# Column products over one pre-added tile in place of four, in a spectral MLP layer on one core: POOL adds the squares, ACT and POOL build two modulation rows

## The chip, the cores and the metric

The kernel runs on one core of a Trainium2 chip. The metric is the time of one execution on the device, in microseconds (us). Engines are named as in the profile: PE (matrix products; PEld is its weight load), DVE (vector), ACT (scalar and activation functions), POOL (the general-purpose SIMD engine), SP (it issues the DMAs). Each engine works through its own instructions in the order in which the program holds them; between engines, semaphores make one wait for another.

## The reference

One layer with adaptive normalisation, a spectral block and a gated MLP, over 8192 positions of 448 channels. Cut to what matters:

```python
mod = (silu(c) @ w_mod).reshape(1, 6, 1, -1)
sa, ca, ga, sb, cb, gb = (mod[:, q] for q in range(6))     # six rows of 448
h = layernorm(x) * (1 + ca) + sa
x = x + ga * A(h, w1, b1, w2, b2)     # rfft over positions, a complex two-layer block MLP, irfft
h = layernorm(x) * (1 + cb) + sb
x = x + gb * ((gelu(h @ w_gate) * (h @ w_up)) @ w_down)    # w_gate, w_up: 448 x 1792
```

The kernel computes `w_gate` and `w_up` products in 16-bit halves, for which it scales the weights by powers of two. To choose these it wants an upper bound on the norm of every column of `w_gate` and `w_up` (`nrm`: sums of squares down the 448 rows).

## The kernel before, in words

There are three stages, one after the other. The first (to about 95 us in the trace) reads `x`, normalises it and does the first part of the transform; its result goes to DRAM (`td`). The second (about 95 to 407 us) is the spectral block. The third is the gated MLP, in which PE is busy nearly all the time.

The change lies in the second stage. It treats 32 units (a half `h` of the channels and one of 16 groups `bt` of frequencies) in a software pipeline. `step(i)` works on several units at once, and the order of its calls is the order of the instructions on every engine (the scheduler is switched off here):

- `fetch_t(i+2)`: SP issues the loads of a unit (`tr`), then the hook "load"
- the hook "pe", which stands ahead of all other PE work of the step
- `stage_s2(i)`: PE makes the second transform (`ps`, L344 to L346, 24 products); ACT (`zh`, L352) and DVE (`zl`, L353) write it as two halves
- `split_t(i+1)`: ACT writes `th` and POOL writes `tl` for the next unit
- the hook "act"
- `stage_m2(i-2)`, twice: PE makes the second MLP layer (`pm`, L417 to L422, 12 products each time); DVE clips it (`t`, L430) and writes `y` (L438); `split_y` lets ACT write `yh` (L99) and POOL write `yl` (L101)
- `stage_i1(i-3)`: PE makes the inverse transform (`pi`, L467 to L469); ACT copies it (`us`, L470), and SP stores it (`vd`)
- the hook "dve"
- `stage_m1(i-1)`: PE makes the first MLP layer (`pm`, L390 to L395, 24 products); ACT (`hh`, L407) and DVE (`hl`, L408) write it as two halves
- the hook "pool", which stands behind all other POOL work of the step

The function `at(i, hook, fn, ...)` hangs side work into these hooks. In steps 1 to 16 this is the work on the weights' norms. `load_w` brings 256 columns of `w_gate` or `w_up` (`raw`: 448 rows as three tiles of 128 rows and one of 64, that one twice). One step later `squares` (ACT, L633) writes the squares in bf16 (`sq`, four tiles of 256 columns). Another step later `norms` multiplies each tile's columns with a column of ones on PE (L642, 4 tiles by 2 halves of 128 columns are 8 products) and adds them up in PSUM (`pw`); `norms_out` (DVE, L649) scales the sum by a bound's margin. There are 14 such pieces, in steps 3 to 16.

`mod_row` makes a modulation row, the same on all 128 partitions: for each half of 224 columns, four f32 products of silu(c) (`cs`), spread over 128 columns, with the four tiles of 112 rows of `w_mod` (L606, 8 products; the trace shows an f32 product as two, so 16). It stands in the hook "pe" of step 6 for the row `cb` and of step 8 for `sb`; ACT copies the result (L609). The rows `ga` and `gb` are made after the loop in the same way.

The tiles `raw` come from a pool of eight buffers and `sq` from four.

Of the kernel before, what the change touches and what calls it, by code (L numbers as in the profile page):

```python
# [10 lines left out]
F32 = mybir.dt.float32  # L11
# [4 lines left out]
AF = mybir.ActivationFunctionType  # L16
ALU = mybir.AluOpType
# [6 lines left out]
HC = 224  # L24
# [17 lines left out]
def spectral_geglu(ctx, tc, x, w1, b1, w2, b2, wg, wu, wd, cvec, wmod, cf1, cs2, cmi, cgm, out):  # L42
    nc = tc.nc
    V, S, G, T = nc.vector, nc.scalar, nc.gpsimd, nc.tensor
# [9 lines left out]
    cpool = ctx.enter_context(tc.tile_pool(name="cpool", bufs=1))  # L54
    psum = ctx.enter_context(tc.tile_pool(name="psum", bufs=2, space=bass.MemoryType.PSUM))

    def bank(tag, name):
        return psum.tile([128, 512], F32, tag=tag, name=name)
# [4 lines left out]
    make_identity(nc, ident)  # L63
    onesb = cpool.tile([128, 2], BF16, name="onesb")
    V.memset(onesb, 1.0)
    ga_r = cpool.tile([128, D], F32, name="ga_r")
    gb_r = cpool.tile([128, D], F32, name="gb_r")
    cb_r = cpool.tile([128, D], F32, name="cb_r")
    sb_r = cpool.tile([128, D], F32, name="sb_r")
    cs = cpool.tile([112, 4], F32, name="cs")  # L70
    nrm = cpool.tile([128, 2, NFT], F32, name="nrm")
# [56 lines left out]
    with ExitStack() as actx:  # L128
# [18 lines left out]
        q, y, t, nm, mu = (ap.tile([128, NB], F32, name=nm) for nm in ("q", "y", "t", "nm", "mu"))  # L147
# [117 lines left out]
        pe, start = 0.0, {}  # L265
        for g, bs in enumerate(groups):
# [5 lines left out]
            at = [pos[0] + 0.06] + [pos[i] + d for i in (1, 2, 3) for d in (0.03, 0.06)] + [pos[3] + 0.1]  # L272
            if g == 0:
                at = [t_stats[e] + 0.2] + [pos[0] + 0.03] * 7
            for t_, f in zip(at, scale_steps(bs)):
                ex(t_, f)
            for bb in bs:
                pe = start[bb] = max(pe + 0.75, at[-1] + 0.3)
# [20 lines left out]
    with ExitStack() as bctx:  # L299
# [200 lines left out]
        def at(i, hook, fn, *args):  # L500
            side.setdefault((i, hook), []).append((fn, args))
# [80 lines left out]
        raws = {}  # L582
# [16 lines left out]
                out.append(wm)  # L599
            return out  # L600

        def mod_row(key, dst=None):
            ps = bank("pd", "psm")
            for hh, wm in enumerate(raws.pop(key)):
                for k in range(4):
                    T.matmul(ps[:, hh * HC : (hh + 1) * HC], cs[:, k : k + 1].to_broadcast([112, 128]), wm[:, k, :], start=k == 0, stop=k == 3)  # L606
            if dst is None:
                return ps[:, :D]
            S.copy(dst, ps[:, :D])  # L609
# [21 lines left out]
        def squares(pr, j):  # L631
            sq = npool.tile([128, 4, 256], BF16, tag="sq", name="sq", bufs=4)
            S.activation(sq, raws.pop(("n", pr, j)), AF.Square)  # L633
            raws[("q", pr, j)] = sq

        def norms(pr, j):
            sq = raws.pop(("q", pr, j))
            ps = bank("pd", "pw")
            for f in range(2):
                for t in range(4):  # L640
                    kr = 128 if t < 3 else 64
                    T.matmul(  # L642
                        ps[:, f : f + 1], sq[:kr, t, f * 128 : (f + 1) * 128], onesb[:kr, 0:1], start=t == 0, stop=t == 3
                    )
            raws[("s", pr, j)] = ps

        def norms_out(pr, j):
            ps = raws.pop(("s", pr, j))
            V.tensor_scalar(nrm[:, pr, 2 * j : 2 * j + 2], ps[:, 0:2], 1.02, 1e-30, op0=ALU.mult, op1=ALU.add)  # L649

        def all_max(dst, src, n, first=(), then=()):

# [100 lines left out]

        nctx = ExitStack()
        npool = nctx.enter_context(tc.tile_pool(name="npool", bufs=1))
        at(3, "load", pre, npool, "cb", load_mod_row, 4)
        at(5, "load", pre, npool, "sb", load_mod_row, 3)
        at(6, "pe", mod_row, "cb", cb_r)
        at(8, "pe", mod_row, "sb", sb_r)
        for n in range(14):  # L760
            j, pr = divmod(n, 2)
            at(1 + n, "load", pre, npool, ("n", pr, j), load_w, pr, j)
            at(2 + n, "act", squares, pr, j)
            at(3 + n, "pe", norms, pr, j)
            at(3 + n, "pe", norms_out, pr, j)
        for j in range(7):
# [106 lines left out]
        drain()  # L873
        down_weights(0, G)
        mod_row("ga", ga_r)
        assert not tiny
    mctx.close()
# [406 lines left out]
```

## Time and profile before

| | |
|---|---|
| median of 3 runs | 2001.53 us (2000.57 to 2001.66) |
| the profiled execution | 2000.8 us |
| its span in the trace | 1999.0 us |
| PE busy | 1928.4 us, 96% of the span |
| DVE, ACT, POOL busy | 1155.3, 769.1 and 1198.8 us |
| mean granted clock of PE | 0.985 of full speed |

The span is what the trace covers; the execution's own time lies 1.8 us above it, and 0.7 us under the median. The busy shares are means over three stages that have different limits, so the table alone does not say what a change in the second stage is worth.

### The profile page before, as it was taken

To read this page: it belongs to the slowest core of one execution; us is meant where nothing else is said; L and a number is where in the kernel's file an instruction comes from. 1 tells how busy PE (TensorE), PEld (TensorE's weight loads), DVE (VectorE), ACT (ScalarE), POOL (GpSimd) and SP (SyncE) were. 2 spreads that over 40 slices of the span, in tenths; PEclk is the share of its full clock that TensorE was granted. 3 is DMA by queue.
4 is the path that set the end of the run, shared out by engine and by line. 5 is a ranking of instruction groups with operands and counts; after the bars stand their busy time and mean duration, and the time that the engine had idled before them with its cause. 6 is when DMAs were issued, how large, how long until landed. Compare 5 with 4: busy or idle time off the path is not lost.

```text
span 1999.0 us, 43611 instructions
## 1 busy us (share of the span) xinstructions
PE 1928.4 (96%) x17678; PEld 1709.9 (86%) x17678; DVE 1155.3 (58%) x2419; ACT 769.1 (38%) x1293; POOL 1198.8 (60%) x1492
## 2 busy tenths in 40 slices
PE   6799989977999999999999999999999999999999
PEld 3498989966898988888888888888888888889898
DVE  6578888867555555555554555555555555555533
ACT  3566667653333333333333333333333333333322
POOL 3444446557666666666666666666666666666644
PEclk8899999988999999999999999999999999999999
DMA  9886667731111111111111111111111111111000
GB/s 389 288 224 161 174 154 192 191 91 50 47 43 43 42 44 43 42 48 46 42 45 51 42 42 42 42 49 44 42 42 42 42 42 43 43 42 44 22 17 20
DMA packets 165570, 157.74 MB, mean 79 GB/s; under 512 B 86388, under 2 KB 146424, under 8 KB 165368
## 3 DMA queue, kind: packets, MB, share of 16 engines
q1 hardware_dynamic: 165368, 154.94, 27.1%
q8 instruction: 139, 2.28, 0.5%
q14 instruction: 63, 0.52, 0.1%
HBM read 95.09 MB, written 44.04 MB: 70 GB/s over the span
## 4 chain that ended last, share of the span: by engine, by line
PE 81%; DVE 9%; DMA 4%; ACT 2%; POOL 1%; SPq 1%; issue 1%; ACTq 0%; DVEq 0%; POOLq 0%
PE pgu L1016 49%; PE pdn L1084 7%; PE pdn L1083 7%; PE pdn L1082 7%; DVE y L438 2%; DMA td<-st 2%; PE ps L186 1%; DMA raw<-in_B_w_up 1%; DVE zl L353 1%; PE pi L916 1%; DVE hl L408 1%; DVE t L430 1%; PE pi L914 1%; PE pi L915 1%; PE ps L344 0%
## 5 line engine op out<-in xcount | busy, mean ns | idle before, releaser
L1016 PE MATMUL pgu<-nt,wh 128*128 128x256 f16 x6272 | 834.4, 273 | 1.2 <-DVE x L1057 1.2
L1016 PEld LDWEIGHTS <-wh 128*128 128x128 f16 x6272 | 602.9, 98 | 99.1 <-issue 31.3
L1052 ACT ACTIVATE gel<-pgu,dg 128x256 f32<-128x256 f32 x448 | 200.2, 473 | 790.7 <-PE pgu L1016 750.9
L1016 PE MATMUL pgu<-nt,wl 128*128 128x256 f16 (+1 forms) x3584 | 502.1, 272 | 1.8 <-DVE x L1057 1.7
L1082 PE MATMUL pdn<-wd,ac 128*128 128x224 f16 x1568 | 407.7, 260 | 4.3 <-DVE x L925 2.3
L1084 PE MATMUL pdn<-wd,ac 128*128 128x224 f16 x1568 | 407.8, 260 | 0.2 <-DVE ac L1075 0.2
L1083 PE MATMUL pdn<-wd,ac 128*128 128x224 f16 x1568 | 407.8, 260 | 0.0
L1063 POOL TENSOR_TENSOR x<-x 128x128 f32<-128x128 f32 x223 | 240.1, 1077 | 234.2 <-DVE x L1057 234.2
L1075 DVE SCALAR_TENSOR_TENSOR ac<-x,sa_act,ac 128x896 f16<-128x896 f32 (+1 forms) x225 | 311.7, 1385 | 81.6 <-ACT ac L1074 81.6
L1016 PEld LDWEIGHTS <-wl 128*128 128x128 f16 (+1 forms) x3584 | 297.9, 97 | 59.6 <-issue 26.4
L1057 DVE TENSOR_TENSOR x<-pgu,gel 128x256 f32<-128x256 f32 x448 | 179.6, 418 | 283.1 <-ACT gel L1052 282.5
L1074 ACT ACTIVATE ac<-x,sa_act 128x896 f16<-128x896 f32 (+1 forms) x225 | 232.9, 1035 | 53.2 <-POOL x L1066 51.3
L1117 POOL TENSOR_TENSOR o<-u,p 128x224 f32<-128x224 f32 x32 | 21.1, 658 | 292.8 <-DVE u L1116 292.8
L1064 POOL TENSOR_TENSOR x<-x 128x128 f32<-128x128 f32 x223 | 158.4, 710 | 17.5
L1083 PEld LDWEIGHTS <-ac 128*128 128x128 f16 x1568 | 154.1, 98 | 5.4 <-issue 4.7
L1082 PEld LDWEIGHTS <-ac 128*128 128x128 f16 x1568 | 154.1, 98 | 1.0 <-issue 0.2
L1084 PEld LDWEIGHTS <-ac 128*128 128x128 f16 x1568 | 154.1, 98 | 0.9 <-DVE ac L1075 0.5
L101 POOL TENSOR_TENSOR yl<-y,yh 128x448 fp32r<-128x448 f32 x63 | 75.0, 1190 | 88.6 <-ACT yh L99 86.4
L1065 POOL TENSOR_TENSOR x<-x 128x128 f32<-128x128 f32 x223 | 112.3, 504 | 0.0
L1066 POOL TENSOR_TENSOR x<-x 128x128 f32<-128x128 f32 x223 | 108.1, 485 | 0.0
L101 POOL TENSOR_TENSOR tl<-tr,th 128x896 f16<-128x896 f32 x30 | 57.3, 1909 | 80.0 <-ACT th L99 41.1
L438 DVE TENSOR_TENSOR y<-pm,t 64x224 f32<-64x224 f32 x256 | 99.4, 388 | 8.5 <-DVE t L430 0.5
(304 smaller groups left out, 2831.9 us busy)
## 6 DMA issues: line engine op xcount, KB each, us to landing
td<-st SPq DMA_DIRECT2D x16, 896.0 KB, 9.7
tr<-td SPq DMA_DIRECT2D x64, 224.0 KB, 4.4
vd<-us SPq DMA_DIRECT2D x64, 224.0 KB, 2.8
xx<-in_A_x SPq DMA_DIRECT2D x32, 448.0 KB, 3.5
v<-vd SPq DMA_DIRECT2D x64, 224.0 KB, 2.8
out<-x SPq DMA_DIRECT2D x31, 448.0 KB, 2.7
xt<-in_A_x SPq DMA_DIRECT2D x15, 896.0 KB, 16.9
nt<-pk SPq DMA_TRANSPOSE x480, 2.4
```

The costliest lines, as they stand in the source:

```text
L101: (el or V).tensor_tensor(lo, src, h, ALU.subtract)
L438: V.tensor_tensor(y[ri * 64 : ri * 64 + 64, gi], pv[si, ri], tv[si, ri], ALU.subtract)
L1016: T.matmul(pgu[i, t, q][:, pr * H : (pr + 1) * H], w[rows, tw, f0 : f0 + 128], nts[i][rows, tn, :], start=start, stop=stop, skip_group_che ...
L1052: S.activation(gl, ps[:, :H], AF.Gelu_apprx_tanh, scale=dg)
L1057: V.tensor_tensor(dst, ps[:, H : 2 * H].rearrange("p (b c) -> p b c", b=2), gl.rearrange("p (b c) -> p b c", b=2), ALU.mult)
L1063: e.tensor_tensor(s1, a21, a22, ALU.add)
L1064: e.tensor_tensor(s2, s1, a11, ALU.subtract)
L1074: S.activation(ac[:, 0, k], x[:, k], AF.Copy, scale=sc)
L1075: V.scalar_tensor_tensor(ac[:, 1, k], x[:, k], sc, ac[:, 0, k], op0=ALU.mult, op1=ALU.subtract)
L1082: T.matmul(ps, ac[:, 0, ka], wds[t][:, 0, kb], start=t == 0, stop=False)
L1083: T.matmul(ps, ac[:, 0, ka], wds[t][:, 1, kb], start=False, stop=False)
L1084: T.matmul(ps, ac[:, 1, ka], wds[t][:, 0, kb], start=False, stop=t == NP - 1)
```

## The change

The weights' squares: a new `square_sums`, in the hook "pool" of the step that squares, adds the four bf16 tiles of `sq` into the first with three POOL additions, in place. `norms` then makes two products on the one tile, where it made eight. The margin in `norms_out` goes from 1.02 to 1.04, since the sums are rounded to bf16.

The rows `cb` and `sb`: they are loaded one step earlier (steps 2 and 4). For each half of the row, a new `mod_prods` lets ACT multiply the four tiles with `cs` in place, in the hook "act", and a new `mod_sums` lets POOL add the four into one with two additions, in the hook "pool" (steps 4 and 5 for `cb`, 6 and 7 for `sb`). `mod_row` then makes one f32 product for each half, with a tile of ones (`onesf`), in the same steps 6 and 8 as before. `ga` and `gb` stay as they are.

```diff
+    onesf = cpool.tile([112, 128], F32, name="onesf")
+    V.memset(onesf, 1.0)
...
+        def mod_prods(key, hh):
+            wm = raws[key][hh]
+            for k in range(4):
+                S.activation(wm[:, k, :], wm[:, k, :], AF.Copy, scale=cs[:, k : k + 1])
+
+        def mod_sums(key, hh):
+            wm = raws[key][hh]
+            G.tensor_tensor(wm[:, 0:2], wm[:, 0:2], wm[:, 2:4], ALU.add)
+            G.tensor_tensor(wm[:, 0], wm[:, 0], wm[:, 1], ALU.add)
+
-        def mod_row(key, dst=None):
+        def mod_row(key, dst=None, summed=False):
...
+                if summed:
+                    T.matmul(o, onesf, wm[:, 0, :], start=True, stop=True)
+                    continue
...
+        def square_sums(pr, j):
+            sq = raws[("q", pr, j)]
+            G.tensor_tensor(sq[:64, 2], sq[:64, 2], sq[:64, 3], ALU.add)
+            G.tensor_tensor(sq[:, 0], sq[:, 0], sq[:, 1], ALU.add)
+            G.tensor_tensor(sq[:, 0], sq[:, 0], sq[:, 2], ALU.add)
...
-                for t in range(4):
-                    kr = 128 if t < 3 else 64
-                    T.matmul(
-                        ps[:, f : f + 1], sq[:kr, t, f * 128 : (f + 1) * 128], onesb[:kr, 0:1], start=t == 0, stop=t == 3
-                    )
+                T.matmul(ps[:, f : f + 1], sq[:, 0, f * 128 : (f + 1) * 128], onesb[:, 0:1], start=True, stop=True)
...
-        at(3, "load", pre, npool, "cb", load_mod_row, 4)
-        at(5, "load", pre, npool, "sb", load_mod_row, 3)
-        at(6, "pe", mod_row, "cb", cb_r)
-        at(8, "pe", mod_row, "sb", sb_r)
+        for i, key, q, dst in ((2, "cb", 4, cb_r), (4, "sb", 3, sb_r)):
+            at(i, "load", pre, npool, key, load_mod_row, q)
+            for hh in range(2):
+                at(i + 2 + hh, "act", mod_prods, key, hh)
+                at(i + 2 + hh, "pool", mod_sums, key, hh)
+            at(i + 4, "pe", mod_row, key, dst, True)
...
+            at(2 + n, "pool", square_sums, pr, j)
```

The next two lists show POOL's instructions in steps 4 and 5. `tl` is the split of the next unit, the two `yl` are the two splits of the MLP's output; lines in the changed kernel are two or more higher. Before:

```order
L101 TENSOR_TENSOR tl_1295<-tr_1088,th_1294 128x896
L101 TENSOR_TENSOR yl_1321<-y_1315,yh_1320 128x448
L101 TENSOR_TENSOR yl_1358<-y_1339,yh_1357 128x448
L101 TENSOR_TENSOR tl_1447<-tr_1241,th_1446 128x896
L101 TENSOR_TENSOR yl_1473<-y_1467,yh_1472 128x448
L101 TENSOR_TENSOR yl_1510<-y_1491,yh_1509 128x448
```

In the changed kernel, the same place (step 4 and the first instruction of step 5):

```order
L103 TENSOR_TENSOR tl_1295<-tr_1097,th_1294 128x896
L103 TENSOR_TENSOR yl_1325<-y_1319,yh_1324 128x448
L103 TENSOR_TENSOR yl_1362<-y_1343,yh_1361 128x448
L613 TENSOR_TENSOR raw_966<-raw_966 112x2x224
L614 TENSOR_TENSOR raw_966<-raw_966 112x224
L657 TENSOR_TENSOR sq_1302<-sq_1302 64x256
L658 TENSOR_TENSOR sq_1302<-sq_1302 128x256
L659 TENSOR_TENSOR sq_1302<-sq_1302 128x256
L103 TENSOR_TENSOR tl_1446<-tr_1243,th_1445 128x896
```

Three additions of squares, and in steps 4 to 7 two more for a modulation row ahead of them, now stand behind the second `yl` of the step.

The second place is PE at the change from step 5 to step 6. `w1h`, `w1l`, `zh` and `zl` belong to the last products of `stage_m1`. Before:

```order
L393 MATMUL pm1_1530<-zh1_803,w1h_92 112x256
L394 MATMUL pm1_1530<-zl_1291,w1h_92 112x256
L395 MATMUL pm1_1530<-zh1_803,w1l_93 112x256
L606 MATMUL psm_1557<-raw_1091,cs_78 128x224 x4
L606 MATMUL psm_1557<-raw_1093,cs_78 128x224 x4
L642 LDWEIGHTS sq_1450
L642 MATMUL pw_1567<-onesb_72,sq_1450 128x1
```

In the changed kernel:

```order
L396 MATMUL pm1_1533<-zl_1291,w1h_94 112x256
L397 MATMUL pm1_1533<-zh1_805,w1l_95 112x256
L621 MATMUL psm_1565<-raw_966,onesf_74 128x224
L621 MATMUL psm_1565<-raw_968,onesf_74 128x224
L665 LDWEIGHTS sq_1453
L665 MATMUL pw_1569<-onesb_72,sq_1453 128x1
```

The last pair of rows stands eight times in a row before and twice now; behind it come the products of `stage_s2` of step 6 in both. What PE reads there now (`raw_966`, `raw_968`, `sq_1453`) was last written by POOL.

More of the change, by code (lines that the diff above doesn't have):

```diff
@@ L600, in load_mod_row @@
             return out
-        def mod_row(key, dst=None):
+        def mod_prods(key, hh):
[7 more added lines that the diff above has]
+        def mod_row(key, dst=None, summed=False):
             ps = bank("pd", "psm")
             for hh, wm in enumerate(raws.pop(key)):
+                o = ps[:, hh * HC : (hh + 1) * HC]
+                if summed:
+                    T.matmul(o, onesf, wm[:, 0, :], start=True, stop=True)
+                    continue
                 for k in range(4):
-                    T.matmul(ps[:, hh * HC : (hh + 1) * HC], cs[:, k : k + 1].to_broadcast([112, 128]), wm[:, k, :], start=k == 0, stop=k == 3)
+                    T.matmul(o, cs[:, k : k + 1].to_broadcast([112, 128]), wm[:, k, :], start=k == 0, stop=k == 3)
             if dst is None:
@@ L648, in norms_out @@
             ps = raws.pop(("s", pr, j))
-            V.tensor_scalar(nrm[:, pr, 2 * j : 2 * j + 2], ps[:, 0:2], 1.02, 1e-30, op0=ALU.mult, op1=ALU.add)
+            V.tensor_scalar(nrm[:, pr, 2 * j : 2 * j + 2], ps[:, 0:2], 1.04, 1e-30, op0=ALU.mult, op1=ALU.add)
         def all_max(dst, src, n, first=(), then=()):
```

## The prediction

> **What bounds the kernel now.** I read the chain that ended last first, then the stretch in which the change works, then one step of it in the timeline. The stretch goes from the first product of `norms` (step 3) to the last (step 16). Columns of the second row: stretch, length, busy time of PE, PEld, DVE, ACT, POOL, then PE's granted clock, DMA share, GB/s.
>
> ```profile
> PE 81%; DVE 9%; DMA 4%; ACT 2%; POOL 1%; SPq 1%; issue 1%; ACTq 0%; DVEq 0%; POOLq 0%
> 113.98:240.78 126.80, 124.09 (x1182) 119.45 (x1180) 106.26 (x233) 80.84 (x137) 57.17 (x72) 1.00 0.75 190
> PE ps L344 <- DVE hl L402: 1.7, 2, 1.0
> PE pm1a L390 <- DVE y L449: 0.6, 1, 0.6
> ```
>
> PE bounds this stretch: 124.09 of 126.80 us busy at full clock, and its waits come to hardly more than the 1.7 and 0.6 us of the two rows from the list of waits. POOL is busy 57 of 127 us. From these shares alone the change looks good: it moves work from the full engine to a half-idle one. What decides is the moment at which POOL is free, and that is in the timeline. Step 5 begins at 131.84 us, step 6 at 140.59 (start, length, engine, line, and at the end what a wait was for):
>
> ```profile
> 131.84 0.60 PE L642 MATMUL pw<-onesb,sq 128*128 128x1 bf16 x8
> 132.37 0.26 PE L344 MATMUL ps<-s,th 128*112 128x128 f16 x1
> 133.34 1.36 ACT L352 ACTIVATE zh<-ps,ca 112x512 fp32r<-112x512 f32 x2 [0.39 <-PE ps L346]
> 134.07 1.42 DVE L353 SCALAR_TENSOR_TENSOR zl<-ps,ca,zh 112x512 fp32r<-112x512 f32 x2 [0.21 <-ACT zh L352]
> 135.03 0.27 PE L422 MATMUL pm<-w2h,hl 112*128 112x224 f32 x1
> 135.40 0.61 DVE L430 TENSOR_SCALAR t<-pm 128x448 f32<-128x448 f32 x1
> 136.12 1.59 DVE L438 TENSOR_TENSOR y<-pm,t 64x224 f32<-64x224 f32 x4
> 137.75 0.62 DVE L430 TENSOR_SCALAR t<-pm 128x448 f32<-128x448 f32 x1
> 137.80 0.57 ACT L99 CAST yh<-y 128x448 fp32r<-128x448 f32 x1 [1.32 <-DVE y L438]
> 138.47 1.59 DVE L438 TENSOR_TENSOR y<-pm,t 64x224 f32<-64x224 f32 x4
> 140.16 0.57 ACT L99 CAST yh<-y 128x448 fp32r<-128x448 f32 x1 [0.92 <-DVE y L438]
> 140.59 3.19 PE L606 MATMUL psm<-raw,cs 112*128 112x224 f32 x16
> 140.80 1.14 POOL L101 TENSOR_TENSOR yl<-y,yh 128x448 fp32r<-128x448 f32 x1 [1.20 <-ACT yh L99]
> 143.61 0.59 PE L642 MATMUL pw<-onesb,sq 128*128 128x1 bf16 x8
> ```
>
> DVE goes without a break from 134.07 to the end of the second `y` (140.06), then ACT makes `yh` and POOL `yl`. So POOL's last work of step 5 ends at 140.80 + 1.14 = 141.94, when PE already stands in step 6. That costs nothing before, as PE needs this `yl` only in `stage_i1` of step 6; it is a lag of 1.35 us behind PE.
>
> **The change part by part.** *What PE saves.* Eight products of `norms` take 132.37 - 131.84 = 0.53 us, 0.066 each. Two take 0.13, with a weight load of about 0.1 in front once PE stands still: 0.25. A modulation row takes 143.61 - 140.59 = 3.02 us for 16 passes; four would take 0.76. In all 14 x 0.40 + 2 x 2.27 = 10.1 us, if PE stays the bound.
>
> *What it adds on PE's path.* The new additions stand on POOL behind the second `yl`, and the hook "pe" of the next step, ahead of all its other products, reads their result. PE works in order, so `stage_s2` and everything after it queue behind that wait. The lag therefore becomes a wait, and the additions' own time comes on top. How often and how far POOL lags, first and last of 14 steps:
>
> ```profile
> 115.18 1.15 POOL L101 TENSOR_TENSOR yl<-y,yh 128x448 fp32r<-128x448 f32 x1 [1.12 <-ACT yh L99]
> 113.98 0.23 PE L642 MATMUL pw<-onesb,sq 128*128 128x1 bf16 x3
> 241.00 1.14 POOL L101 TENSOR_TENSOR yl<-y,yh 128x448 fp32r<-128x448 f32 x1 [1.20 <-ACT yh L99]
> 240.78 0.33 PE L642 MATMUL pw<-onesb,sq 128*128 128x1 bf16 x4
> ```
>
> From the end of `yl` back to the first instruction of the hook this is 2.35 us at step 3 and 1.36 at step 16. The 14 lags (shortest 1.14, at step 12) add up to 23.1 us.
>
> For the additions there is no bf16 row. The nearest on POOL (mean ns is the second number behind the bar; the last column is idle time before):
>
> ```profile
> L101 POOL TENSOR_TENSOR gl<-g,gh 128x256 fp32r<-128x256 f32 x32 | 23.9, 746 | 7.1 <-ACT gh L99 7.1
> L978 POOL TENSOR_TENSOR pk<-n,pk 128x128 f16<-128x128 f32 x31 | 13.4, 431 | 8.1 <-ACT pk L971 8.1
> L835 POOL TENSOR_TENSOR dr<-dr 128x224 f32<-128x224 f32 x2 | 1.7, 844 | 0.0
> L837 POOL TENSOR_TENSOR raw<-raw 128x224 f32<-128x224 f32 x2 | 1.3, 672 | 0.2
> L828 ACT CAST wd<-raw 128x224 f16<-128x224 f32 x2 | 0.7, 373 | 0.0
> ```
>
> `gl` has the very size, 746 ns; additions in place (L837) are 672 for 224 columns with 0.1 us between dependent ones. I take 0.68 each, a little under `gl` for the narrower type, and 0.1 between: 2.15 us. Lower end 3 x 0.43 = 1.3 (half the columns), upper end 3 x 0.844 + 0.2 = 2.7 (the slow case beside a busy DVE).
>
> Each step then starts later by its lag + 2.15 + 0.05 (hand-over) - (0.53 - 0.25), which is lag + 1.92: over 14 steps 23.1 + 26.9 = 50.0 us.
>
> *The modulation rows.* In steps 4 to 7 two more additions stand ahead of the squares on POOL: 448 columns as `yl` (1.14) and 224 (0.67), 1.9 us with the gap, all on the same path: + 7.6. The products L606 no longer hold steps 6 and 8: - 2 x 3.02; their four passes run while POOL adds squares. ACT's four scalings, 4 x 0.373 = 1.5 us, stand ahead of the squares and the first `yh`, before which ACT waited 1.32 us; the 0.2 left over goes into the 0.92 before the second `yh`. Nothing; without that cover 4 x 1.5 = 6. PE's waits on DVE of 1.7 and 0.6 us fall into the new waits: - 2.3. Sum so far: 50.0 + 7.6 - 6.0 - 2.3 = 49.3 us.
>
> *The loads* of `cb` and `sb` come a step earlier, 0.8 MB each row, ahead of that step's weight loads on SP; at 190 GB/s that is 4.2 us of transfer, in steps that become over 3 us longer. Nothing; if a `tr` lands late for it, up to 4 us once. The memset of `onesf` is one DVE instruction (a `t` takes 0.62) before the first data are there: nothing.
>
> *The clock.* In a plain step PE works from 132.37 to 140.59, 8.2 us, and the new loop is 9.57 (132.37 to 141.94) + 2.15 + 0.05 + 0.25 = 12.0 us. PE now stands still some 3.5 us in every step. What the trace shows after waits:
>
> ```profile
> 484.59 0.26 PE L1084 MATMUL pdn<-wd,ac 128*128 128x224 f16 x1
> 487.13 0.26 PE L1082 MATMUL pdn<-wd,ac 128*128 128x224 f16 x1 [2.28 <-DVE x L925]
> 487.61 0.39 PE L1084 MATMUL pdn<-wd,ac 128*128 128x224 f16 x1
> 490.97 0.28 PE L1084 MATMUL pdn<-wd,ac 128*128 128x224 f16 x1
> 283.88 0.37 PE L417 MATMUL pm<-w2h,hh 113*128 113x224 f32 x1 [1.09 <-ACT hh L407]
> 284.82 0.27 PE L420 MATMUL pm<-w2h,hh 112*128 112x224 f32 x1
> 284.93 0.28 PE L421 MATMUL pm<-w2l,hh 112*128 112x224 f32 x1
> 286.31 0.41 PE L418 MATMUL pm<-w2l,hh 113*128 113x224 f32 x1
> 286.53 0.41 PE L419 MATMUL pm<-w2h,hl 112*128 112x224 f32 x1
> 448.12 0.93 PE L1016 MATMUL pgu<-nt,wh 128*128 128x256 f16 x7 [1.17 <-DVE x L1057]
> 450.00:455.00 5.00, 4.93 (x47) 3.88 (x45) 4.48 (x9) 1.04 (x1) 4.76 (x7) 1.00 0.48 171
> ```
>
> After a wait of 2.28 us the products slow down from 487.61 to 490.97, 3.4 us. After 1.09 us (and a little more) they stand 0.22 us apart instead of 0.11, about 0.52 of the pace; after 1.17 us at 448.12 the clock stays at 1.00. So waits of 3.5 us should bring a slow phase in nearly every step. It hurts where DVE waits for PE: `t` at 135.40 starts right behind the twelfth `pm` product (135.03 + 0.27), 2.93 us after the step's first product. A slow phase of 3.4 us from that first product does 1.75 us of work, so `t` and all behind it come 1.65 us later: 14 x 1.65 = 23.1. Bounds: nothing, where no slow phase falls there, and 2.93 / 0.52 - 2.93 = 2.7 in every step, 38 us. I take the middle one, since one slow phase is what the rows show after one wait.
>
> Sum: 49.3 + 23.1 = 72.4 us, on the profiled execution's 2000.8 (span 1999.0) 2073.2; the median of the runs stands 0.7 above that, so 2074.
>
> [...]
>
> **The rivals.** *The same waits, the clock stays up.* For it speaks the row at 448.12; against it the two slow phases. 2000.8 + 49.3 + 0.7 = 2051. Chance 0.22. [...]
>
> *POOL is done in time and PE keeps its gain:* 10.1 us less, 1991. It needs the sums to end before PE leaves `stage_m1`: at step 6, 141.94 + 2.15 against 140.59, so POOL would have to be 3.5 us earlier. `yl` would have to wait less, but its chain is DVE's unbroken row from 134.07, which the change leaves alone. Chance 0.05.
>
> *The delay is given back behind step 16.* What follows is PE-bound or waits on DVE, and nothing there starts at a fixed time; giving back 70 us would need a stage that is bound by transfers, and DMA is busy 0.75 even here. About 2002. Chance 0.03.
>
> *Dearer still:* slow additions and slow phases over the whole of 2.93 us, 49.3 + 0.55 x 14 + 38 = 95 us, 2096 or more. Chance 0.08.
>
> **How the numbers follow.** The forecast, 2060 to 2094, has 0.6. With the first rival the range is 2040 to 2094 (0.82); its lower end is also the sum without slow phases and with additions of 1.3 us, 49.3 - 0.85 x 14 = 37.4, 2039. A change of this kernel is seen above about 0.2%, 4 us. Slower by more: 0.6 + 0.22 + 0.08 and 0.02 for sums between 2006 and 2040, 0.92; within: 0.03; faster: 0.05.
>
> **What the profile would show.** Right: in the list of waits, PE or PEld at `pw` waiting for POOL `sq`, 14 times, 3 to 4 us each, longer where a modulation row is added; the second `yl` of successive plain steps 12 to 14 us apart where the steps were 8.75 (131.84 to 140.59); the 14 steps' granted clock clearly under 1.00; the third stage as long as before. Wrong: no such waits, or POOL's additions far from 0.68 us; a clock of 1.00 between the waits (first rival); or a chain from `zl` to `yl` that is shorter than 9.57 us when PE no longer runs ahead.

## The result: 3% slower, and the profile after

The changed kernel takes 2063.98 us (median of 4 runs, 2060.9 to 2064.4), the kernel before 2001.6 on the same chip: a ratio of 1.0305, 95% interval 1.0293 to 1.0318. 62.4 us are lost. The profiled execution took 2064.07 us, its span is 2062.2, 63.2 above the span before.

The page's summary of the chain that ended last (POOL has 3% of it, where it had 1%), then the stretch from the first product of `norms` to the last (columns as in the prediction):

```profile
PE 78%; DVE 10%; DMA 4%; POOL 3%; ACT 2%; issue 1%; SPq 1%; DVEq 0%; ACTq 0%; POOLq 0%
```

```profile
119.58:302.45 182.87, 136.26 (x1079) 130.56 (x1079) 108.83 (x231) 87.23 (x152) 89.15 (x118) 0.86 0.51 130
```

The stretch grew from 126.80 to 182.87 us, by 56.1. PE executes 103 instructions fewer in it and yet is busy 12 us longer, as its granted clock fell from 1.00 to 0.86; and it now stands still for 46.6 us, where it stood still for 2.7. The other 7.1 us of the span: the first `norms` starts 5.6 us later (its first wait is 4.23), and 1.5 come after the stretch.

What PE waits for from 105 to 305 us (total us, times, longest; beside these two only 0.2 us):

```profile
PE pw L665 <- POOL sq L659: 45.8, 14, 5.0
PE psm L621 <- POOL raw L614: 5.1, 2, 2.6
```

All 14 `norms` wait for POOL's last addition. The end of step 8 and the start of step 9, as the timeline has it (start, length, engine, line; rows of POOL and of PE):

```profile
204.70 1.13 POOL L103 TENSOR_TENSOR yl<-y,yh 128x448 fp32r<-128x448 f32 x1 [1.20 <-ACT yh L101]
205.78 0.66 POOL L657 TENSOR_TENSOR sq<-sq 64x256 bf16<-64x256 bf16 x1
206.41 0.66 POOL L658 TENSOR_TENSOR sq<-sq 128x256 bf16<-128x256 bf16 x1
207.15 0.67 POOL L659 TENSOR_TENSOR sq<-sq 128x256 bf16<-128x256 bf16 x1
207.87 0.21 PE L665 MATMUL pw<-onesb,sq 128*128 128x1 bf16 x2 [3.54 <-POOL sq L659]
207.94 0.33 PE L346 MATMUL ps<-s,th 128*112 128x128 f16 x1
208.28 0.31 PE L346 MATMUL ps<-s,th 128*112 128x128 f16 x1
208.60 0.31 PE L346 MATMUL ps<-s,th 128*112 128x128 f16 x1
```

This is the step of the prediction: `yl` ends at 205.83, the additions follow without a break, PE reads 0.05 us after the last one (207.82), and everything of step 9 queues behind. Two of three `ps` products lie between neighbouring rows here; they are 0.32 us apart, at a granted clock of 0.50 from 207.9 to 211 us, where they are 0.17 apart at a granted clock of 1.00 (265.63 to 265.80, shown in the last section).

The third stage did not give anything back. Its gate and up products, before and after (the two numbers behind the durations are the first and the last start):

```profile
L1016 PE MATMUL pgu<-nt,wh x6272: 269/273/421, 425.1 to 1979.3; 128*128 128x256 f16 x196
```

```profile
L1040 PE MATMUL pgu<-nt,wh x6272: 269/273/421, 488.5 to 2042.5; 128*128 128x256 f16 x196
```

1554.2 us before, 1554.0 after.

### The profile page after: what moved, and what is told of

Its sections match the earlier page's. It is cut to its first block, busy times and chain, and to the rows that moved or that the text cites. A ratio compares the mean times of both kernels' runs of the same rounds, so it can differ in the third digit from the quotient of the medians.

```text
span 2062.2 us, 43473 instructions
## 1 busy us (share of the span) xinstructions
PE 1942.4 (94%) x17570; PEld 1722.5 (84%) x17570; DVE 1157.4 (56%) x2420; ACT 775.2 (38%) x1309; POOL 1233.2 (60%) x1542
## 4 chain that ended last, share of the span: by engine, by line
PE 78%; DVE 10%; DMA 4%; POOL 3%; ACT 2%; issue 1%; SPq 1%; DVEq 0%; ACTq 0%; POOLq 0%
PE pgu L1040 49%; PE pdn L1108 7%; PE pdn L1106 7%; PE pdn L1107 7%; DVE y L440 4%; DMA td<-st 2%; DVE t L432 1%; PE ps L188 1%; DVE zl L355 1%; DMA xt<-in_A_x 1%; POOL yl L103 1%; PE pi L940 1%; DVE hl L410 1%; DMA raw<-in_B_w_up 1%; PE ps L346 1%
```

## The experiments

My theory: the loss is the place of the new additions, not their amount. They stand behind the second `yl`, where POOL lags PE, and PE's first instruction of the next step reads them; the waits then throttle PE's clock (0.86 in the stretch). Rivals: the modulation rows carry much of it; the clock has no part in it; POOL simply has too much to do. Each kernel is the changed one with one edit. In summary (the kernel before took 2002.3, 2002.65 and 2002.06 us beside the first four, the next three and the last):

| edit | us | ratio to before, 95% interval |
|---|---|---|
| 1 modulation rows alone | 2005.55 | 1.0019 (1.0009 to 1.0028) |
| 2 squares alone | 2052.17 | 1.0251 (1.0237 to 1.0265) |
| 3 sums read late in the step | 2013.1 | 1.0060 (1.0047 to 1.0073) |
| 4 PE kept busy in the wait | 2052.73 | 1.0255 (1.0241 to 1.0269) |
| 5 as 3, with a free PSUM bank | 2006.69 | 1.0021 (1.0012 to 1.0030) |
| 6 sums ahead of the step's `yl` | 1997.45 | 0.9974 (0.9966 to 0.9983) |
| 7 one addition of three | 2035.25 | 1.0160 (1.0145 to 1.0176) |
| 8 as 5, the rows' products at their old place | 1998.71 | 0.9986 (0.9977 to 0.9995) |

**1 and 2: each part alone.** For the rows alone `norms` has its eight products back and `square_sums` is not called:

```diff
-                T.matmul(ps[:, f : f + 1], sq[:, 0, f * 128 : (f + 1) * 128], onesb[:, 0:1], start=True, stop=True)
+                for t in range(4):
+                    kr = 128 if t < 3 else 64
+                    T.matmul(
+                        ps[:, f : f + 1], sq[:kr, t, f * 128 : (f + 1) * 128], onesb[:kr, 0:1], start=t == 0, stop=t == 3
+                    )
...
-            at(2 + n, "pool", square_sums, pr, j)
```

> Only the modulation rows are built the new way; the norms make their eight products as before. Theory W (POOL's lag behind PE turns into a wait in front of the step, and slow clock follows the wait): two waits, at steps 6 and 8, each 1.35 us of lag plus 1.83 us of additions, against 3.02 us of products saved: +0.6 us a step, +1.2 in all, and up to 1.7 more each where the clock drops: 2002 to 2006 us. Rival P (POOL's additions cost their own time wherever their result is read): four pairs of 1.83 us, +7 us, 2009 or more.

For the squares alone the rows are made as before:

```diff
-        for i, key, q, dst in ((2, "cb", 4, cb_r), (4, "sb", 3, sb_r)):
-            at(i, "load", pre, npool, key, load_mod_row, q)
-            for hh in range(2):
-                at(i + 2 + hh, "act", mod_prods, key, hh)
-                at(i + 2 + hh, "pool", mod_sums, key, hh)
-            at(i + 4, "pe", mod_row, key, dst, True)
+        at(3, "load", pre, npool, "cb", load_mod_row, 4)
+        at(5, "load", pre, npool, "sb", load_mod_row, 3)
+        at(6, "pe", mod_row, "cb", cb_r)
+        at(8, "pe", mod_row, "sb", sb_r)
```

> Only the squares are added on POOL; the modulation rows make their eight products as before. Theory W: 14 waits of about 3.4 us; the old products of the rows run inside the waits of steps 6 and 8 and cost nothing, so the only thing that goes against the changed kernel is the rows' additions, 4 x 1.83 = 7.3 us: 2057 us. If the rows' products don't fit into the waits, 6 us more, 2063. Rival P: the same 2057, so this run tells the parts' sizes and not the theories.

The rows alone cost 3.3 us, the squares alone 49.9. PE's waits on POOL, rows alone and then squares alone:

```profile
PE psm L621 <- POOL raw L614: 5.4, 2, 2.7
```

```profile
PE pw L665 <- POOL sq L659: 41.1, 13, 4.3
```

The rows wait in two steps only (2.7 us each) and save products there, so they nearly pay for themselves; that is within what was expected. The squares alone came 4.8 us lower than expected. Together the parts cost 62.4, 9 more than the sum of each alone. Most of that is the rows' additions standing ahead of the squares on POOL, which neither part has alone: the 14 gaps from a second `yl` to the next step's first `ps` product add up to 37.3 us in the changed kernel and to 29.9 with the squares alone.

**3: read the same sums late in the step.** PE asks for them behind `stage_i1`, some 5.5 us later; the last `norms` stays where it was. Nothing else changes, POOL's order least of all.

```diff
-            at(i + 4, "pe", mod_row, key, dst, True)
+            at(i + 4, "dve", mod_row, key, dst, True)
...
-            at(3 + n, "pe", norms, pr, j)
-            at(3 + n, "pe", norms_out, pr, j)
+            hook = "dve" if n < 13 else "pe"
+            at(3 + n, hook, norms, pr, j)
+            at(3 + n, hook, norms_out, pr, j)
```

> All of the change stays, but PE reads the sums behind the inverse transform of the same step instead of ahead of everything (13 of 14 norms and both rows; the last norm stays where it was, since the scales need it). Theory W: the sums end some 2.9 us (4.8 with a row) into the step, PE comes to them after 5.2 us, so 13 of 14 waits go: 13 x 0.40 + 4.5 us saved, one wait of 3.4 and up to 1.7 of slow clock left: 1997 us, from 1994 to 2000. Rival P: POOL's additions delay tl and yl wherever they are read, 30 us or more remain: above 2015.

50.9 us of the 62.4 go, but the time was to end below the kernel before, and stands 10.8 above it; neither theory W nor rival P foretold this. PE's longest waits from 105 to 305 us:

```profile
PE pw L665 <- ACT us L472: 14.0, 11, 3.1
PE psm L621 <- ACT us L472: 3.6, 2, 2.2
PE pi L469 <- ACT us L472: 2.3, 1, 2.3
PE pw L665 <- POOL sq L659: 2.0, 1, 2.0
```

The wait on POOL is gone (only the last `norms`, unmoved, has one), and a new one stands in its place that I had overlooked: `pw` and `psm` are written into the same pair of banks of PSUM (the memory that takes PE's products) as `pi`, and right behind `stage_i1` ACT is still copying `pi` out of them (`us`). The third row, one wait of `pi` itself, is there before the change too.

**4: keep PE busy in the wait.** 24 products of an identity matrix, whose result nobody reads, stand ahead of the two of `norms`; all sums and waits stay.

```diff
+            for _ in range(24):
+                T.matmul(ps[:, 128:256], identb, identb, start=True, stop=True, skip_group_check=True)
```

> The changed kernel with 24 small products of the identity ahead of each norm, in the wait, into columns that nobody reads; they add no result. Theory W with the clock: PE doesn't idle, the clock stays up, and the loop from a step's first product to the end of the second yl goes back to 9.6 us in plain steps: 13 to 15 us less than the changed kernel, 2049 to 2051 us. Rival K (the clock plays no part, the longer loop comes from ACT or DVE): 2064 us or more.

11.3 us less, with 24 more products in each of 14 steps; 13 to 15 were expected. The filler covers only a part of the wait: PE still stands idle for 28.7 us ahead of `norms`, where it stood for 45.8.

```profile
PE pw L667 <- POOL sq L659: 28.7, 12, 3.7
```

The stretch from its first `norms` to its last:

```profile
120.46:294.12 173.66, 142.71 (x1390) 137.12 (x1391) 107.79 (x231) 86.76 (x152) 89.24 (x118) 0.93 0.53 138
```

The granted clock is 0.93 where it was 0.86, and the stretch 9.2 us shorter. What changed is the chain from a step's first `ps` product to the end of its second `yl`: over steps 3 to 15 it sums to 137.7 us against 147.7 in the changed kernel and 134.6 before, and five of the steps are back at the 9.56 us of before. In plain steps the time from that `yl` to the next step's first product is the same 2.11 us. So the additions cost what they cost, and these chains are 13.1 us longer on top; the filler regains 10.0 of that, not all, as slow phases remain in steps 3, 5, 7 and 15 (chains of 11.0 to 11.1 us, granted clock 0.79 over their first 8.3 us).

**7: one addition of three.** `square_sums` keeps only the last one, so this kernel leaves the second tile's and the half tile's squares out of the norms.

```diff
-            G.tensor_tensor(sq[:64, 2], sq[:64, 2], sq[:64, 3], ALU.add)
-            G.tensor_tensor(sq[:, 0], sq[:, 0], sq[:, 1], ALU.add)
```

> Two of the three additions of squares are left out (the norms then miss two tiles); all else as in the changed kernel. Theory W: each wait is shorter by two additions, 1.36 us as they start 0.62 and 0.74 us apart: 14 x 1.36 = 19 us less, 2045 us, and a little less where the clock recovers sooner. If the wait were the lag of yl alone: 2064 us.

```profile
PE pw L663 <- POOL sq L657: 27.7, 12, 3.7
```

From `yl` to the next step's first product it takes 0.75 us in place of 2.11, so two additions are 1.36 us of every step, as the price from the trace said. But the kernel is 28.7 us faster than the changed one, not 19. The additions account for 14 x 1.36 = 19. The chains to the second `yl` account for 7.8 more (139.9 us over steps 3 to 15 against 147.7): four of the steps are back at 9.49 to 9.56 us, with 27.7 us of waits in place of 45.8 and a granted clock of 0.976 over the profiled execution, where the changed kernel has 0.971. Still 32.6 us of the loss remain with a single addition of 0.67 us a step. These additions make 9.4 of them and the rows' additions 7.3; the rest, about half, is POOL's lag and what it does to the clock, less what the saved products give back.

**5 and 8: the late read, with its banks mended.** In 5 the sums and the rows go to another bank (its tag is that of the MLP's second layer `pm`, free again by then), the rest is as in 3:

```diff
-            ps = bank("pd", "psm")
+            ps = bank("pc" if summed else "pd", "psm")
...
-            ps = bank("pd", "pw")
+            ps = bank("pc", "pw")
```

> As the run that reads the sums behind the inverse transform, but the norms and rows take their PSUM bank from the pair that the second MLP layer uses, whose earlier reader (DVE) is done by then, instead of the pair that ACT is still copying. If that run's 20 us of PE waiting on ACT's copies were its bank and nothing of theory W: 1997 us, from 1993 to 2001. If POOL's additions themselves hold the step up (rival P): no better than 2013.

6.4 us better than 3, and still 10 above the expectation. Its plain steps do what was hoped: 8.44 to 8.47 us from one step's first `ps` product to the next, against 8.75 before. But the two steps with a modulation row take 12.65 and 14.99 us. In these PE waits 1.4 us between the row's products and `norms`; the likely reason is that the row has taken the new bank. In step 8 it also stands still for 1.8 us ahead of the row's products. These two rows are from the timeline of step 6:

```profile
146.98 0.99 PE L621 MATMUL psm<-raw,onesf 112*128 112x224 f32 x4 [0.30 <-PE pi L471]
149.38 0.19 PE L665 MATMUL pw<-onesb,sq 128*128 128x1 bf16 x2 [1.41 <-DVE y L440]
```

and the clock falls behind it (columns as above; step 6 and step 8):

```profile
141.22:153.87 12.65, 10.94 (x86) 10.21 (x85) 8.19 (x17) 8.52 (x16) 11.54 (x13) 0.87 0.93 252
162.32:177.31 14.99, 11.75 (x86) 11.02 (x85) 9.95 (x23) 7.04 (x12) 12.08 (x30) 0.78 0.85 220
```

Kernel 8 puts that to the test: as 5, but the rows' products stand at the step's start, in their old bank, and POOL adds the rows ahead of the step's first `yl`.

```diff
-            ps = bank("pc" if summed else "pd", "psm")
+            ps = bank("pd", "psm")
...
-                at(i + 2 + hh, "pool", mod_sums, key, hh)
-            at(i + 4, "dve", mod_row, key, dst, True)
+                at(i + 2 + hh, "act", mod_sums, key, hh)
+            at(i + 4, "pe", mod_row, key, dst, True)
```

> The kernel with the norms read late from a free bank (2006.7 us), but the two rows' single products stand at the step's start again, in the bank they had before, and POOL adds the rows ahead of the step's first yl. In that kernel the two steps with a row took 12.65 and 14.99 us where their neighbours took 8.45, with a wait of 1.4 us at pw behind the row's products and a granted clock of 0.87 and 0.78. Theory: the row in the norms' new bank is the whole of its miss, and goes: 10.7 us less, 0.8 us for each row's own products back, so about 1997.5 (1995 to 2000), and steps 6 and 8 of 9 to 10 us. Rival: the miss lies in reading the norms late at all (waits at pw on DVE's y in other steps): then 2004 to 2007 stays.

8.0 us less than 5, within the range expected, and a little faster than before (0.14%). From one step's first `ps` product to the next, the two stretches that hold a row's products now take 9.2 us, and the one between them 8.8. What still waits is the norms, for DVE's `y`, and for POOL in the last piece, which reads early:

```profile
PE pw L665 <- DVE y L440: 3.6, 5, 1.2
PE pw L665 <- POOL sq L659: 3.0, 1, 3.0
```

**6: the same sums, earlier in POOL's queue.** Read where the change reads them; POOL adds in the hook "act", behind `tl` and ahead of the step's two `yl`, and no longer in the hook "pool".

```diff
-                at(i + 2 + hh, "pool", mod_sums, key, hh)
+                at(i + 2 + hh, "act", mod_sums, key, hh)
...
-            at(2 + n, "pool", square_sums, pr, j)
+            at(2 + n, "act", square_sums, pr, j)
```

> The changed kernel with all of POOL's additions moved ahead of the step's two yl, right behind tl, where POOL used to wait for ACT; same instructions, same reader in the same place. Theory W: in a plain step the sums end at about 7.2 us after the step's first product (tl ends 5.1, additions 2.03) and PE comes to them at 8.2, so nothing waits; with a row they end 0.8 us late, in four steps, part of it under the row's passes. PE keeps its 10.1 us less 2 to 3: 1994 us, from 1991 to 1998. Rival P (POOL's additions cost their time wherever they stand): 28 us and more above before, 2030.

This is the fastest of all: 1997.45 us, 0.26% under the kernel before. POOL in the last step of the stretch, and PE's `norms` before and behind it:

```profile
226.57 0.20 PE L665 MATMUL pw<-onesb,sq 128*128 128x1 bf16 x2
230.03 1.91 POOL L103 TENSOR_TENSOR tl<-tr,th 128x896 f16<-128x896 f32 x1 [1.83 <-ACT th L101]
231.90 0.67 POOL L657 TENSOR_TENSOR sq<-sq 64x256 bf16<-64x256 bf16 x1
232.53 0.68 POOL L658 TENSOR_TENSOR sq<-sq 128x256 bf16<-128x256 bf16 x1
233.28 0.68 POOL L659 TENSOR_TENSOR sq<-sq 128x256 bf16<-128x256 bf16 x1
233.91 1.15 POOL L103 TENSOR_TENSOR yl<-y,yh 128x448 fp32r<-128x448 f32 x1
234.95 0.20 PE L665 MATMUL pw<-onesb,sq 128*128 128x1 bf16 x2
235.51 1.14 POOL L103 TENSOR_TENSOR yl<-y,yh 128x448 fp32r<-128x448 f32 x1 [0.44 <-ACT yh L101]
```

The last addition ends at 233.96, 1 us before PE wants it; the two `yl` move back by what the additions take, and lie beside PE's next step, where nobody waits for them yet. The step is 8.38 us long, 0.37 under the 8.75 of before; the clock is 1.00 in the stretch, and 1.4 us in two waits is all that `norms` still waits for POOL:

```profile
115.01:234.95 119.94, 114.35 (x1078) 109.59 (x1079) 105.36 (x232) 85.30 (x153) 89.47 (x119) 1.00 0.78 201
```

```profile
PE pw L665 <- POOL sq L659: 1.4, 2, 0.8
```

With the very same instructions the ratio to before is 0.9974 here and 1.0305 in the changed kernel, so POOL does not simply have too much to do. The gain of 5.2 us is half of the 10.1 that the products saved are worth by the prediction, and the time 3.5 us above the middle of what I expected; in the profiled execution the stretch is 6.9 us shorter and the third stage begins 3.8 us earlier, so part of it is given back between the two. Step 16 begins 6.3 us earlier than before and step 18 only 3.4: in step 17 PE waits 1.8 us for ACT's `hh`, a wait that the kernel before does not have there, and the granted clock is 0.80 against 0.88. Why `hh` is late there stays open. Which of kernels 6 and 8 is the faster is not shown either; the intervals of their ratios just overlap.

## Why the prediction was right, point by point

*PE is in order, and POOL lags it (23.1 us).* Right. In all 14 steps `norms` waits for the last addition, 2.7 to 5.0 us (1.3 in steps 6 and 8, where the row's products have waited ahead of it). Kernels 3 and 5, which leave POOL alone and move the reader, and 6, which leaves the reader alone and moves POOL's work, take nearly all of that wait away (1.4 to 3.0 us remain), and with it 51 to 67 us.

*Three additions of 0.68 us and the gaps, 2.15, with the hand-over and PE's restart 2.45.* Right in kind, 0.35 too dear. All additions of the run (shortest, median, longest in ns, first and last start):

```profile
L657 POOL TENSOR_TENSOR sq<-sq x14: 658/662/903, 117.5 to 300.4; 64x256 bf16<-64x256 bf16 x14
L658 POOL TENSOR_TENSOR sq<-sq x14: 656/659/662, 118.1 to 301.0; 128x256 bf16<-128x256 bf16 x14
L659 POOL TENSOR_TENSOR sq<-sq x14: 665/666/667, 118.9 to 301.7; 128x256 bf16<-128x256 bf16 x14
```

From the end of `yl` to the end of the third it is 1.99 us (205.83 to 207.82), and the next `ps` starts 0.12 behind that; so 2.11 us lie between `yl` and this product, and as much in seven other plain steps (2.36 and 2.27 behind steps 9 and 10). That a busy DVE slows an addition, as the upper end of 2.7 has it, was not shown: the two of L835 on POOL took 0.66 us (at 451.50 in the trace of before) and 1.03 (at 460.01), with DVE busy beside both, for 0.61 of 0.65 and 1.01 of 1.05 us. All 14 gaps, those with a row included, add up to 37.3 us, where the prediction's prices make it 14 x 2.45 + 7.6 = 41.9: 4.6 us of the miss.

*The modulation rows, + 7.6 - 6.0.* Right: with a row the gap is 3.94 us, 1.83 more than without, in four steps 7.3 (forecast 1.9 each). This row is from the turn to step 7; it waits 1.45 us longer than the 3.54 of step 9 above:

```profile
178.48 0.21 PE L665 MATMUL pw<-onesb,sq 128*128 128x1 bf16 x2 [4.99 <-POOL sq L659]
```

*The clock, 23.1 us.* Right that it slows (0.86 of full speed in the stretch, 1.00 before), and nearer to the middle value taken than to either end; some 6 us too dear. The chains from first product to second `yl` sum to 147.7 us over 13 steps, against 134.6 before: 13.1 more, where the prediction makes it 13 x 1.65 less the 2.3 us of old waits on DVE, 19.2. The steps scatter. Five (4, 11, 12, 13, 15) lose 1.3 to 1.6 us, near the 1.65 taken; 5 and 7, behind the longest waits, lose 2.4; 3, 6 and 8 lose 0.6 to 1.1. Steps 9 to 11 were long before the change already (11.28, 14.01 and 11.59, at a granted clock of 1.00), so that 9 loses nothing and 10 gains, and step 14 had no slow phase at all (1.00 from 277.5 to 289). That the sum comes so near is in part luck, as what lies above and below the middle value cancels.

*ACT's scalings and the earlier loads, put at nothing.* Right. In kernel 4 the clock holds in steps 4 and 6, and these take the 9.56 us of a plain step although each has four scalings; and from 105 to 305 us PE waits for no load.

*The rival "the clock stays up", 2051.* Refuted: granted clock 0.86, and kernel 4 regains 11 us without taking a wait's cause away.

*The rivals "POOL is done in time" and "given back".* Both refuted in this kernel, by the 14 waits and by the third stage's 1554.0 us. But the first names what kernel 6 makes true: it needed POOL 3.5 us earlier, I looked only at the chain that feeds `yl`, and the additions do not depend on `yl` at all.

The two terms that were too large, by 4.6 and some 6 us, make up the distance from 2074 to 2064; against them some 1.5 us came on top elsewhere, as the span grew by 63.2 us where 72.4 were forecast. The time lies 4 us above the lower end of the forecast.

## What to carry to other kernels

Before moving work from the engine that bounds a loop to a half-idle one, look up in the timeline how far that engine lags the reader, at the reader's very instruction: the lag becomes a wait, even if the work added is small (here lags of 1.14 to 2.35 us, with additions of 1.99 and 1.83 more for a row, became waits of 2.7 to 5.0). Then choose the place in the helper's queue: the same additions cost 62 us behind a late instruction and gained 5 ahead of it. A reader that is moved instead brings its PSUM bank along; check whose copies that bank waits for at the new place (in kernel 3 `norms` waited 14.0 us for ACT's).

## What the runs showed of the hardware that I had not expected

- POOL's additions in place took 0.66 us for 64 partitions (L657, median of 14) as for 128 (L658; both of 256 bf16 columns): here fewer partitions made an addition no shorter.
- When the slow phase comes after a wait varies. After waits of 3.12 and 2.96 us the next steps start like this (rows of `ps`, three products apart; the first two are of step 13, the last of step 14):

```profile
265.63 0.22 PE L346 MATMUL ps<-s,th 128*112 128x128 f16 x1
265.80 0.27 PE L346 MATMUL ps<-s,th 128*112 128x128 f16 x1
278.81 0.22 PE L346 MATMUL ps<-s,th 128*112 128x128 f16 x1
```

 Step 13 begins at 264.60 at full pace and slows 1.2 us later (granted clock 1.00 up to 265.8, 0.50 from there to 269); step 9 was slow from its first product (207.94; 0.50 up to 211); step 14, from 277.61, stays at 1.00 over 3.5 us:

```profile
277.50:281.00 3.50, 3.45 (x44) 3.45 (x45) 1.87 (x4) 2.43 (x4) 0.17 (x1) 1.00 1.04 286
264.50:268.00 3.50, 3.46 (x35) 3.47 (x36) 1.66 (x3) 2.31 (x4) 0.03 (x1) 0.69 0.74 173
```

 So in these steps a wait near 3 us slowed PE mostly, not always, and the delay is not fixed to the wait's end. Of steps 3 to 15 twelve were slow (granted clock 0.67 to 0.83 over their first 8.3 to 8.9 us), five of them behind waits of 2.73 to 3.31 us; step 14, behind one of 2.96, was not. What decides it was not shown.
